# Sigmoid attention and mixture of depths: choosing matmuls moved and halved, values over five gaps, q and k turned behind the outputs

## Chip, cores and metric

One NeuronCore of a Trainium2 chip runs the whole kernel. The metric is the device time of one execution in microseconds. Before the change the median of three runs is 466.48 us (465.75 to 466.99). The execution that the profile shows has a span of 467.6 us.

## What is computed

Eight batches of 448 tokens go through an attention of twelve heads of width 64, in which the softmax is replaced by a sigmoid. The outputs of the heads, side by side, are rows of 768. In each batch the 128 rows with the highest gate score then go through a two-layer network and are added to themselves, weighted by the sigmoid of the score; all other rows pass unchanged.

```python
scores = scale * np.matmul(q, k.transpose(0, 1, 3, 2)) - np.log(S)
attn = 1.0 / (1.0 + np.exp(-scores))
x = np.matmul(attn, v)                  # then (B, H, S, D) -> (B, S, H * D)
...
gate = np.einsum('bsd,d->bs', x, w_gate)
out = x.copy()
for b in range(B):
    top_idx = np.argpartition(-gate[b], capacity)[:capacity]     # capacity = 128
    xe = x[b, top_idx]
    ye = np.maximum(xe @ w1, 0.0) @ w2                           # 768 -> 1024 -> 768
    g = 1.0 / (1.0 + np.exp(-gate[b, top_idx]))
    out[b, top_idx] = xe + g[:, None] * ye
```

Everything is float32.

## The kernel before

**Steps and units.** The 8 x 12 heads are 24 groups of four (`NQ`), taken two at a time in 12 steps `s` (`NS`). Three groups make a batch, so a batch ends in the middle or at the end of a step. A step has seven units `n` (`NU`). A unit (L287) multiplies q and k for a slice of the key tokens, 16 matmuls that the trace records as 32, into two PSUM tiles of two banks each, and ScalarE turns both tiles into the sigmoid (L311). The first matmul of a unit waits until ScalarE has read the tiles' earlier contents. There are four such tiles: two of the pool "psc", and o0 and o1, which collect a step's outputs and are also lent to other work. Some units use o0 and o1 in place of psc (L290): units 1, 3 and 5 of step 0 and unit 4 of steps 1 to 3.

**Values.** `values(s, n)` (L327) is one of four blocks of matmuls that multiply the sigmoids by v into o0 and o1. Blocks 0 and 1 have 64 records, blocks 2 and 3 have 48. Block 0 of step s stands behind the last unit of step s, and blocks 1, 2 and 3 stand behind units 0, 1 and 2 of step s+1. Behind block 3 VectorE transposes the outputs out of o0 and o1 into x_b (`take`, L360, four instructions), which frees the two tiles.

**Order.** The scheduler is manual: each engine executes its instructions in the order in which the Python code emits them. `stream` (L762) emits unit after unit, and `gap(s, n)` (L684) whatever stands behind unit n: value blocks, products of the expert network from the table `WORK` (steps 4 to 11), and what was put off with `put`. TensorE, ScalarE and VectorE each have a queue of this kind; plain loads and stores are issued by SyncE, the scores' and rows' transfers by GpSimd, each in order too.

**VectorE's share.** `turn(i)` (L269) transposes k and q of group i in 32x32 blocks; units 0 to 2 of step s need group 2s, unit 3 and later ones need group 2s+1. `turn(2s+1)` is emitted behind unit 1 of step s, and `turn(2s+2)` behind unit 5. `gates(i)` (L672) multiplies the new outputs by the gate weights and reduces them (L374, L377). When a batch is complete, `gate(b)` (L389) adds this up to one score per token; the scores go to DRAM (L402) and come back spread over all partitions (`spread`, L414). `ranking` (L667) then counts for each token how many are ahead of it (L422, L425) and compares the count with the slot numbers (`place`, L433), which gives the tile `hot`: in column i a one at the token of slot i. In steps 1 to 3 VectorE also makes sums of weight quarters (`make_sum`, L175), for a product scheme with seven products in place of eight.

**Choosing.** `choose(b)` (L438) multiplies `hot`, in four parts of 128 tokens, by `who`, whose two columns hold a token's number and score, into a bank of o0 or o1. Four matmuls (8 records) thus give the token and score of each slot. `fetch` (L447) adds the batch's offset (`idx`, L450), copies the score (`got`, L453) and issues the gather of the 128 rows from DRAM. For batches 0 to 5 this stands behind unit 5 of the step after the one in which the scores were spread; for batch 6 it is in `rest`, the tail behind the last step, ahead of all products there; for batch 7 further down in the tail.

**Fillers.** `keep_busy` (L319) issues four matmuls of no use (three in step 3) behind unit 5 of steps 1 to 3, into the tile that will be o0 of the next outputs.

**Pools of the tail.** `banks("any")` takes tiles of "psc" and of o0 and o1 in turn. A product waits until VectorE or ScalarE has read what its tile held.

Of the kernel before, what the change touches and what calls it, by code (L numbers as in the profile page):

```python
# [17 lines left out]
def kernel(  # L18
# [216 lines left out]
    place_s = const.tile([P, NC], F32, name="place_s")  # L235

    def constants():
        make_identity(nc, iden)
        for a in range(4):
            p = slice(a * TT, (a + 1) * TT)  # L240
            nc.sync.dma_start(
                out=wg_b[p],
                in_=bass.AP(tensor=moe_w_gate.tensor, offset=moe_w_gate.offset + a * TT,
                            ap=[[0, TT], [P, HP], [1, TT]]))
        nc.gpsimd.iota(slots, pattern=[[1, CAP]], base=0, channel_multiplier=0,
                       allow_small_or_imprecise_dtypes=True)

        nc.gpsimd.memset(above, float(S))
        nc.gpsimd.memset(level, 0.0)
        for t in (gate_s, *who):  # L250
            nc.gpsimd.memset(t, 0.0)
        mine = moe.tile([P, NC], F32, name="place")
        for a in range(4):
            nc.gpsimd.iota(mine[a * TT:(a + 1) * TT], pattern=[[1, NC]], base=a * NC,
                           channel_multiplier=TB, allow_small_or_imprecise_dtypes=True)
        every = moe.tile([P, TB, TT], F32, name="rep", bufs=2)
        nc.gpsimd.iota(every, pattern=[[1, TB], [TB, TT]], base=0, channel_multiplier=0,
                       allow_small_or_imprecise_dtypes=True)
        for t in who:
            nc.gpsimd.tensor_copy(t[:, :, 0], mine)  # L260
        for c in range(NC):
            nc.gpsimd.tensor_scalar(
                out=earlier[:, c, :], in0=every.rearrange("p r t -> p (r t)"),
                scalar1=mine[:, c:c + 1], scalar2=None, op0=ALU.is_lt)
# [21 lines left out]

    def unit(s, n):  # L287


        if (s == 0 and n in (1, 3, 5)) or (s in (1, 2, 3) and n == NF + 1):  # L290
            psc = [banks(0), banks(1)]
        else:
            psc = [banks("psc"), banks("psc")]
# [25 lines left out]
    def keep_busy(s):  # L319


        open_outs(s)
        for _ in range(3 if s == 3 else 4):
            nc.tensor.matmul(outs[s][0][:, 0, :HP * TT], iden,  # L324
                             wg_b.rearrange("p h t -> p (h t)"), start=True, stop=True)

    def values(s, n):  # L327
# [11 lines left out]
        if n < 2:  # L339
            at = 4 * (NF - 1)  # L340
            work[at:at] = [(r, None) for r in quads]
        for r, c in work:
            x, pr = divmod(r ^ n, 2)
            rows = slice(r * TT, (r + 1) * TT)
            for j in range(2):
                if c is None:
                    w, a = th[rows, 2 * pr + j, :], attn[s, pr, NF]
                else:
# [3 lines left out]
                                 start=(n == 0 and c == 0), stop=(n == 3 and c == NF - 1))  # L352
        if n < 3:
# [57 lines left out]
    def spread(b, queue=nc.gpsimd):  # L411
        scores = st[b]["scores"]
        rep = st[b]["rep"] = moe.tile([P, S], F32, name="rep", bufs=2)
# [14 lines left out]

    def place(b):
# [6 lines left out]
            in1=place_s.rearrange("p (c o) -> p c o", o=1).to_broadcast([P, NC, CAP]))  # L436

    def choose(b, ps=None):  # L438

        if ps is None:  # L440
            ps = banks("o")[:, 0]
        for c in range(NC):
            nc.tensor.matmul(ps[:CAP, :2], st[b]["hot"][:, c, :CAP], who[b % 2][:, c, :],  # L443
                             start=(c == 0), stop=(c == NC - 1))
        return b, ps

    def fetch(b, ps):  # L447
# [8 lines left out]
        else:  # L456
            xe = moe.tile([P, D], F32, name="xe", bufs=3)
        nc.gpsimd.indirect_dma_start(
            out=xe[:n], out_offset=None, in_=rows_to(b),
            in_offset=bass.IndirectOffsetOnAxis(ap=idx[:n, 0:1], axis=0))  # L460
        st[b].update(idx=idx, xe=xe, picked=got)
# [187 lines left out]
    def routed(b):  # L649
# [14 lines left out]
        if s + 1 < NS:  # L664
            put(s + 1, NU - 2, lambda b: fetch(*choose(b)), b)
# [17 lines left out]

    def gap(s, n):  # L684
        if n < 3 and s > 0:
            values(s - 1, n + 1)
            if n == 2:
                turns[0] = 1
                for i, (m, key) in enumerate(LENT.get(s, ())):
                    lend(m, key, f"d{(s + 1) % 2}{i}")  # L690
                if not turned_next(s):
                    gates(2 * s - 2)
        for item in WORK.get((s, n), ()):
            do(item)
        if n == 3 and turned_next(s):
# [4 lines left out]
        if n == NU - 1 and s < NS:  # L700
            values(s, 0)
        for fn, args in late.pop((s, n), ()):
            fn(*args)
        if n == 3 and s > 0 and not turned_next(s):
# [3 lines left out]
            if waiting:  # L708
                gate(waiting.pop())

    def rest():
# [5 lines left out]
        fetch(*choose(b - 1))  # L717
        for key, slot in (((2, 6), "d10"), ((2, 7), "d11")):
            lend(*key, slot)
        work = [(item, begin(item, "any")) for item in ((1, p, 6), (1, p, 7))]  # L720
        gates(2 * NS - 1)
# [40 lines left out]
    def stream():  # L762
# [14 lines left out]
        for s in range(NS):  # L777
            for n in range(NU):
# [4 lines left out]
                if (n == NU - 1 and s == 0) or (n == 3 and s in (1, 2, 3)):  # L783
                    load_v(s + 1)
                elif n == 3 and s > 4:
                    load_v(s)
                gap(s, n)
                if n == NU - 2 and s in (1, 2, 3):
                    keep_busy(s)
                if n == NU - 2:  # L790
# [9 lines left out]
                if (s, n) == (NS - 1, NU - 1):  # L800
                    for key, slot in (((1, 3), "raw"), ((2, 4), "raw"), ((2, 5), "turned")):
                        lend(*key, slot)
# [34 lines left out]
```

## Time and profile before

| what | us |
|---|---|
| time, median of 3 | 466.48 |
| span in the profile | 467.6 |
| TensorE busy | 451.3 |
| VectorE busy | 293.3 |
| ScalarE busy | 181.8 |
| units (L303), 2,688 records | 170.2 |
| choosing (L443), 64 records | 7.8 |
| fillers (L324), 22 records | 5.4 |
| end of the last matmul, about | 461.6 |

Matmuls are pipelined and overlap, so the time that a group takes of TensorE's path is read better from the distance of the starts than from busy time. In a line of a timeline, the first number is the start in us from the beginning of the span, the second the time taken; an "x4" merges neighbours, and brackets hold the idle time of the engine ahead of the line and what ended it.

### The profile page before, as it was taken

The numbers are of one execution on the slowest core, as the hardware profiler recorded it, in microseconds if no ns is written. First come the engines' busy times: TensorE is split into PE (matmuls) and PEld (weight loads), VectorE is DVE, ScalarE is ACT, GpSimd is POOL, SyncE is SP. The second block draws the span as 40 slices with busy tenths as digits, with TensorE's granted clock in tenths as the row PEclk, the third lists the DMA queues.
The fourth block names the chain that finished last, engine by engine and source line by source line (L and its number), as shares of the span: only waits on it lengthen the run. The fifth ranks groups of instructions, "written<-read, shape, count | busy, mean of one in ns | idle before, by whom it ended". The sixth has DMA issues, their size and how long they took to land.

```text
span 467.6 us, 14444 instructions
## 1 busy us (share of the span) xinstructions
PE 451.3 (97%) x6412; PEld 281.9 (60%) x6412; DVE 293.3 (63%) x631; ACT 181.8 (39%) x237; POOL 32.7 (7%) x54
## 2 busy tenths in 40 slices
PE   8999999979999999999999999999999998999994
PEld 3464745434576755576456764676465738869952
DVE  4308769985642895984643795894742858685372
ACT  3846464624545345324445435324255520102000
POOL 6000000010000000010010000010010001001001
PEclk9999999979999999999999999999999998999998
DMA  8897997989753995994764973993823999611001
GB/s 269 220 313 185 342 347 149 264 197 302 165 193 116 207 192 185 204 215 153 173 227 148 153 202 118 228 213 132 220 102 98 222 181 328 106 34 69 2 0 67
DMA packets 128334, 84.67 MB, mean 181 GB/s; under 512 B 97600, under 2 KB 112064, under 8 KB 128272
## 3 DMA queue, kind: packets, MB, share of 16 engines
q1 hardware_dynamic: 126288, 75.84, 62.2%
q0 software_dynamic: 1984, 7.91, 5.7%
q8 instruction: 50, 0.82, 0.8%
q14 instruction: 12, 0.10, 0.1%
HBM read 63.28 MB, written 20.46 MB: 179 GB/s over the span
## 4 chain that ended last, share of the span: by engine, by line
PE 85%; DVE 8%; DMA 3%; issue 1%; ACT 1%; POOLq 0%; DVEq 0%; ACTq 0%
PE o L351 26%; PE psc L303 23%; PE o L519 13%; PE o L584 11%; PE psc L519 4%; PE psc L584 3%; DVE x_b L366 2%; PE o L303 2%; DMA scores<-total 1%; DVE gate_p L377 1%; DVE scr L374 1%; PE o L775 1%; PE o L443 1%; DMA rep<-scores 1%; PE o L324 1%
## 5 line engine op out<-in xcount | busy, mean ns | idle before, releaser
L303 PE MATMUL psc<-qT,kT 32*64 32x448 f32 x2496 | 155.1, 546 | 0.9 <-ACT attn_u L311 0.9
L311 ACT ACTIVATE attn_u<-psc,bias_s 128x896 f32<-128x896 f32 x86 | 81.9, 1004 | 94.6 <-PE psc L303 94.5
L351 PE MATMUL o<-attn_u,raw_v 32*64 32x448 f32 x960 | 107.8, 536 | 0.8 <-ACT o L354 0.8
L351 PE MATMUL o<-attn_d,raw_v 32*64 32x448 f32 x960 | 106.8, 536 | 0.4 <-ACT o L354 0.4
L303 PEld LDWEIGHTS psc<-qT,kT 32*64 32x64 f32 x2496 | 65.2, 133 | 56.4 <-issue 36.0
L311 ACT ACTIVATE attn_d<-psc,bias_s 128x896 f32<-128x896 f32 x70 | 66.7, 1003 | 47.9 <-PE psc L303 47.9
L366 DVE STREAM_TRANSPOSE x_b<-o 128x448 f32<-128x448 f32 x48 | 26.9, 618 | 81.5 <-PE o L351 77.3
L351 PEld LDWEIGHTS o<-attn_u,raw_v 32*64 32x64 f32 x960 | 45.6, 132 | 20.4 <-issue 12.5
L351 PEld LDWEIGHTS o<-attn_d,raw_v 32*64 32x64 f32 x960 | 43.9, 132 | 18.8 <-issue 14.8
L519 PEld LDWEIGHTS o<-rows_t,w_sb 128*128 128x128 f32 x264 | 30.4, 192 | 4.5 <-issue 1.4
L519 PEld LDWEIGHTS o<-rows_t,attn_d 128*128 128x128 f32 x264 | 30.3, 192 | 3.9 <-DVE scr L374 1.4
L519 PE MATMUL o<-rows_t,w_sb 128*128 128x128 f32 x264 | 31.9, 278 | 0.4 <-DVE rows_t L486 0.3
L519 PE MATMUL o<-rows_t,attn_d 128*128 128x128 f32 x264 | 31.6, 277 | 0.3 <-DVE rows_t L492 0.3
L377 DVE TENSOR_REDUCE gate_p<-scr 128x14 f32<-128x448 f32 x48 | 29.8, 621 | 1.7
L374 DVE TENSOR_TENSOR scr<-x_b,wg_b 128x448 f32<-128x448 f32 x48 | 29.5, 615 | 1.0
L595 DVE SCALAR_TENSOR_TENSOR xe<-o,gate,xe 128x384 f32<-128x384 f32 x37 | 21.1, 611 | 13.4 <-PE o L584 13.3
L278 DVE STREAM_TRANSPOSE kT<-raw_k 128x384 f32<-128x384 f32 x46 | 23.4, 548 | 7.5 <-PE psc L303 3.9
L584 PE MATMUL o<-attn_d,hidden 128*128 128x384 f32 x80 | 27.7, 494 | 0.0
L532 DVE TENSOR_TENSOR hidden<-o,hidden 128x512 f32<-128x512 f32 x24 | 16.0, 687 | 17.9 <-PE o L519 17.7
L535 ACT ACTIVATE hidden<-hidden 128x512 f32<-128x512 f32 x12 | 7.6, 630 | 49.9 <-DVE hidden L532 49.9
L422 DVE TENSOR_SCALAR_CACHE_REDUCE scr<-rep,who 128x448 f32<-128x448 f32 (+1 forms) x32 | 21.5, 671 | 8.6 <-DMA rep<-scores 7.6
L584 PE MATMUL o<-w_sb,hidden 128*128 128x384 f32 x72 | 24.7, 491 | 0.0
(112 smaller groups left out, 476.4 us busy)
## 6 DMA issues: line engine op xcount, KB each, us to landing
attn_d<-sum SPq DMA_DIRECT2D x42, 384.0 KB, 5.5
out_dram<-x_b SPq DMA_DIRECT2D x32, 336.0 KB, 7.7
raw_k<-in_k_dram SPq DMA_DIRECT2D x23, 448.0 KB, 5.3
raw_q<-in_q_dram SPq DMA_DIRECT2D x23, 448.0 KB, 5.9
raw_v<-in_v_dram SPq DMA_DIRECT2D x40, 192.0 KB, 8.1
w_sb<-in_moe_w_dram SPq DMA_DIRECT2D x6, 768.0 KB, 10.9
sum<-hidden SPq DMA_DIRECT2D x6, 768.0 KB, 6.3
rep<-scores POOLq DMA_DIRECT2D x7, 224.0 KB, 4.9
```

The source lines that it names most:

```text
L278: nc.vector.transpose(kT[i][:, e, :HK], sk[:, e, :HK].rearrange("p (m c) d -> p c m d", c=NF))
L303: nc.tensor.matmul(psc[h // 2][y * Dh:(y + 1) * Dh, h % 2, :S], kT[2 * s + x][d, e, r:r + 2, :].rearrange("d r t -> d (r t)"), qT[2 * s + ...
L311: nc.scalar.activation(a, psc[pr][:, :, :S], AF.Sigmoid, bias=bias_s, scale=QK_SCALE)
L351: nc.tensor.matmul(o[x][j * Dh:(j + 1) * Dh, pr, :S], w, a[rows, j, :], start=(n == 0 and c == 0), stop=(n == 3 and c == NF - 1))
L366: nc.vector.transpose(x_tiles[b][:, :, 2 * g + pr, :], outs[s][x][:, pr, :S].rearrange("p (r t) -> p r t", t=TT))
L374: nc.vector.tensor_tensor(out=tmp, in0=x_tiles[b][:, :, hp, :], in1=wg_b[:, hp:hp + 1, :].to_broadcast([P, TB, TT]), op=ALU.mult)
L377: nc.vector.tensor_reduce(out=gate_parts[b][:, :, hp], in_=tmp, axis=AX.X, op=ALU.add)
L422: nc.vector.tensor_scalar(out=junk[:n], in0=rep[:n], scalar1=own, scalar2=0.0, op0=ALU.is_gt, op1=ALU.add, accum_out=above[:n, c:c + 1])
L519: nc.tensor.matmul(ps[:, f, :n], w((t * FH + f) * P, P), x[:, t, :n], start=(t == 0), stop=(t == KH - 1))
L532: nc.vector.tensor_tensor(out=dst, in0=a, in1=b, op=ALU.add)
L584: nc.tensor.matmul(ps[:n, :DH], h[:, t, :n], w(t * DH, DH), start=(t == 0), stop=(t == FH - 1))
L595: nc.vector.scalar_tensor_tensor(out=xe[:n, cols], in0=ps[:n, :DH], scalar=st[b]["gate"][:n, 0:1], in1=xe[:n, cols], op0=ALU.mult, op1=ALU ...
```

## The change

**Fillers.** `keep_busy` is removed.

**Values over five gaps.** In steps 1 to 3 ("early") the first 32 records of block 0 stay behind the last unit of the step whose values they are, its other 32 go behind unit 0 of the next step, and blocks 1, 2 and 3 behind units 1, 2 and 3. The unit that borrows o0 and o1 becomes unit 5.

**q and k.** In steps 1 and 2 `turn(2s+2)` and the load behind it come directly behind the output transposes, ahead of `gates` and `gate`, in step 3 directly behind the fetch of batch 0. All gate work of steps 1 to 3 stands behind unit 4. The v load of the next step moves behind unit 4.

**Choosing moved.** Batch 0 is chosen behind unit 4 of step 3, right behind the output transposes; its gather is issued separately, behind unit 5. Batch 6 is chosen behind products 6 and 7 of the tail, into a tile of "any".

**Choosing halved.** For batches 1 to 5 VectorE adds the four parts of `hot`, each multiplied by its column of `who`, behind `place` (eight instructions of 128x128, two chains of four). Two matmuls with a column of ones, in place of four, then give both columns.

**Buffers.** The spread scores have one buffer in place of two. Two loans of summed weights in step 11 are loaded earlier.

```diff
+    ones = const.tile([P, 1], F32, name="ones")
...
+    def early(s):
+        return 1 <= s <= 3
...
-        if (s == 0 and n in (1, 3, 5)) or (s in (1, 2, 3) and n == NF + 1):
+        if (s == 0 and n in (1, 3, 5)) or (early(s) and n == NF + 2):
             psc = [banks(0), banks(1)]
...
-    def keep_busy(s):
-        open_outs(s)
-        for _ in range(3 if s == 3 else 4):
-            nc.tensor.matmul(outs[s][0][:, 0, :HP * TT], iden,
-                             wg_b.rearrange("p h t -> p (h t)"), start=True, stop=True)
...
+        if part is not None:
+            work = work[8:] if part else work[:8]
...
-        rep = st[b]["rep"] = moe.tile([P, S], F32, name="rep", bufs=2)
+        rep = st[b]["rep"] = moe.tile([P, S], F32, name="rep")
...
+    def added(b):
+        return 0 < b < B - 2
...
+        if not added(b):
+            return
+        st[b]["sums"] = both = moe.tile([P, 2, P], F32, name="sums2")
+        for x in range(2):
+            nc.vector.tensor_scalar(out=both[:, x, :CAP], in0=st[b]["hot"][:, 0, :CAP],
+                                    scalar1=who[b % 2][:, 0, x:x + 1], scalar2=None,
+                                    op0=ALU.mult)
+            for c in range(1, NC):
+                nc.vector.scalar_tensor_tensor(
+                    out=both[:, x, :CAP], in0=st[b]["hot"][:, c, :CAP],
+                    scalar=who[b % 2][:, c, x:x + 1], in1=both[:, x, :CAP],
+                    op0=ALU.mult, op1=ALU.add)
...
+        if added(b):
+            for x in range(2):
+                nc.tensor.matmul(ps[:CAP, x:x + 1], st[b]["sums"][:, x, :CAP], ones,
+                                 start=True, stop=True)
+        else:
+            for c in range(NC):
+                nc.tensor.matmul(ps[:CAP, :2], st[b]["hot"][:, c, :CAP], who[b % 2][:, c, :],
+                                 start=(c == 0), stop=(c == NC - 1))
...
-        if s + 1 < NS:
+        if b == 0:
+            put(s + 1, NU - 1.5, gather, b)
+        elif s + 1 < NS:
             put(s + 1, NU - 2, lambda b: fetch(*choose(b)), b)
...
     def gap(s, n):
-        if n < 3 and s > 0:
+        last = 3 if early(s) else 2
+        if early(s) and n <= last:
+            values(s - 1, n, 1 if n == 0 else None)
+        elif n <= last and s > 0:
             values(s - 1, n + 1)
...
+        if n == last + 1 and s == FIRST:
+            fetch(*choose(0))
+            turn(2 * s + 2)
+            load(2 * s + 4)
-        if n == 3 and turned_next(s):
+        if n == last + 1 and (turned_next(s) or early(s)):
             gates(2 * s - 2)
...
-            values(s, 0)
+            values(s, 0, 0 if early(s + 1) else None)
...
+        if early(s) and n == last and s != FIRST:
+            turn(2 * s + 2)
+            load(2 * s + 4)
...
     def rest():
-        fetch(*choose(b - 1))
         for key, slot in (((2, 6), "d10"), ((2, 7), "d11")):
             lend(*key, slot)
         work = [(item, begin(item, "any")) for item in ((1, p, 6), (1, p, 7))]
+        fetch(*choose(b - 1, bank("any")))
...
-                if n == NU - 2 and s in (1, 2, 3):
-                    keep_busy(s)
-                if n == NU - 2:
+                if n == NU - 2 and not early(s):
                     turn(2 * s + 2)
                     load(2 * s + 4)
```

`FIRST` is 3.

## The prediction

> **What bounds the kernel now.** I read the page's busy shares, then the waits of TensorE, then the timelines of ScalarE and VectorE in steps 1 to 4, then granted clock and busy time in short windows. The page's first two parts:
>
> ```profile
> PE 451.3 (97%) x6412; PEld 281.9 (60%) x6412; DVE 293.3 (63%) x631; ACT 181.8 (39%) x237; POOL 32.7 (7%) x54
> ...
> PE   8999999979999999999999999999999998999994
> ...
> PEclk9999999979999999999999999999999998999998
> ```
>
> TensorE is busy nearly throughout; its hole at slice 8 (93 to 105 us) is also where the granted clock falls. The waits of TensorE name the two holes that matter here:
>
> ```profile
> PE o L324 <- DVE got L453: 3.8, 1, 3.8
> PE o L443 <- DVE x_b L366: 1.5, 1, 1.5
> ```
>
> The first is in step 3: the bank of batch 0's choosing is needed by the filler matmuls (L324), and the two small VectorE instructions that empty it (L450, L453) stand behind all the gate work. The second is in the tail. The clock around both, from the windows (us, TensorE busy, clock, DMA share, GB/s):
>
> ```profile
> 95.00:96.00 1.00, 0.00 (x0) 0.96 0.83 126
> 96.00:97.00 1.00, 0.32 (x1) 0.50 0.94 144
> 102.00:103.00 1.00, 1.00 (x24) 0.62 1.03 190
> 389.00:390.00 1.00, 1.00 (x9) 0.73 0.99 384
> 392.00:393.00 1.00, 1.00 (x7) 0.56 1.02 409
> ```
>
> The clock is halved from 96.0 to 102.8 and from 389.7 to 393.1. The latter made one first-layer product (L519, 24 records) last 4.4 instead of 2.7 us.
>
> Steps 1 to 3 have no expert work, so ScalarE's starts give their rhythm (step 2, units 0 to 6, markers left out):
>
> ```profile
> 50.74 1.90 ACT L311 ACTIVATE attn_d<-psc,bias_s 128x896 f32<-128x896 f32 x2 [1.23 <-PE psc L303]
> 55.25 1.91 ACT L311 ACTIVATE attn_d<-psc,bias_s 128x896 f32<-128x896 f32 x2 [1.26 <-PE psc L303]
> 62.80 1.91 ACT L311 ACTIVATE attn_u<-psc,bias_s 128x896 f32<-128x896 f32 x2 [1.88 <-PE psc L303]
> 65.53 1.91 ACT L311 ACTIVATE attn_u<-o,bias_s 128x896 f32<-128x896 f32 x2 [0.83 <-PE o L303]
> 71.08 1.91 ACT L311 ACTIVATE attn_u<-psc,bias_s 128x896 f32<-128x896 f32 x2 [1.85 <-PE psc L303]
> ```
>
> A unit takes 1.50 us of TensorE, its sigmoid 1.9. Two units in a row on the same two banks are 3.76 us apart (1.9 + 1.5 + about 0.35 of signals); with a full value block (3.0) between, 4.51; the unit that borrows the output banks waits for the four output transposes, 2.73; the next one 1.79. Step 2 lasts 24.90 us, step 3 31.48.
>
> VectorE's own timeline matters most (output transposes, last q transpose before a step's outputs, ranks, comparison that ends the ranking):
>
> ```profile
> 36.58 2.24 DVE L366 STREAM_TRANSPOSE x_b<-o 128x448 f32<-128x448 f32 x4 [13.07 <-PE o L351]
> 57.03 1.07 DVE L285 STREAM_TRANSPOSE qT<-raw_q 128x896 f32<-128x896 f32 x1
> 61.43 2.24 DVE L366 STREAM_TRANSPOSE x_b<-o 128x448 f32<-128x448 f32 x4 [3.33 <-PE o L351]
> 79.33 0.68 DVE L422 TENSOR_SCALAR_CACHE_REDUCE scr<-rep,who 128x448 f32<-128x448 f32 x1
> 86.30 2.24 DVE L366 STREAM_TRANSPOSE x_b<-o 128x448 f32<-128x448 f32 x4
> 106.84 0.68 DVE L422 TENSOR_SCALAR_CACHE_REDUCE scr<-rep,who 128x448 f32<-128x448 f32 x1 [2.32 <-DMA rep<-scores]
> 112.82 0.69 DVE L433 TENSOR_TENSOR hot<-slots,place_s 128x512 f32<-128x512 f32 x1
> ```
>
> From 61.43 to 86.30 it has no idle time: a step's VectorE work, 24.9 us, is as long as the step. So VectorE, not TensorE, sets the pace from step 2 to the outputs of step 3.
>
> **What the Trainium skill says.** "TensorE: Matmul & The Clock Gate", section "What's actually happening", has the clock halved after an idle window of about 3.4 us and restored after a busy one. The trace agrees: low for 3.4 us (389.7 to 393.1) and for twice that (96.0 to 102.8). "DMA: Bandwidth & Descriptors", section "Issuing engines are not separate DMA queues", says that transfers of all issuers share the same engines: the two small score transfers have to share. The trace agrees: the score row took 7.0 us and the spread 4.2 in step 2, 3.5 and 7.8 in step 3. For the new VectorE instructions I use "VectorE: DVE Perf Modes", section on the TRN2 errata: fp32 tensor_tensor takes (N+151)/0.96 ns. At N=512 that is 691; the trace has 687 to 692. At 128 it gives an estimate of 291 ns.
>
> **The change, part by part.**
>
> *Fillers gone* (L324, 22 records): 1.5 us in steps 1 and 2, 2.3 at the low clock in step 3. Steps 1 and 2 become 3.76 (unit 1, now behind only half a block of 1.5) + 4.51 + 3.76 + 3.76 + 2.73 (borrowing moves from unit 4 to 5) + 1.79 + 3.76 (unit 0, behind the other half) = 24.07. That is 0.8 less than 24.90, not 1.5, because half a block does not cover the sigmoid.
>
> *Outputs one gap later.* Step 0's last sigmoid is at 20.11; +3.76 +3.76 +4.51 +3.76 puts unit 3 of step 1 at 35.90, and the value block of 2.25 ends at 38.15. VectorE's transposes start at 38.3, against 36.58. From there to the end of turn(5) the same work stands in the queue, 21.5 us (36.58 to 58.10, 3.04 of it a wait for a store): 59.8. Unit 3 of step 2 needs it and would start at 58.45 (38.15 + 1.50 + 2.73 + 1.79 + 3.76 + 3.76 + 4.51 + 2.25), so TensorE gets a new wait of 1.4. Outputs of step 2: 59.9 + 1.5 + 2.25 + 0.1 = 63.8, against 61.43.
>
> *q and k turned directly behind.* This costs nothing in sum, but moves 2.14 us (43.85 to 45.99) ahead of the gates, so the scores leave 2.14 later. They landed just in time before (79.3), so ranking starts 0 to 2.1 later; I take 1.0. Outputs of step 3: 63.8 + 24.9 + 1.0 = 89.7, against 86.30 and against 87.8 when TensorE would be ready.
>
> *Choosing of batch 0 right behind these outputs.* It starts when the first bank is free, 90.9, takes 0.8, idx and got 0.3 after the transposes end at 91.9: unit 5 starts at about 92.4, where before nothing began before 96.68. Unit 0 of step 4 at 92.4 + 1.5 + 1.79 + 4.56 = 100.3, against 107.12. This is the part that works, 6.8 us on TensorE, if VectorE could follow.
>
> *VectorE up to the outputs of step 4.* Before, from 86.30 to the end of the comparison 113.5, 27.2, of which 2.3 waiting: 24.9 of work. New: the eight sums of batch 1, dependent on each other in two chains; 8 x 0.30 = 2.4 (bounds 1.6 and 2.7). The scores leave 2.4 later behind outputs, so the wait for the spread is 1.3 with short transfers, 4.8 with those of before; I take 2.5. Outputs of step 4: 89.7 + 24.9 + 2.4 + 2.5 = 119.5 (116 to 122), against 117.76. Behind these transposes waits the first row transposition (L480), which needs their bank: 120.7, against 119.05. Before, TensorE idled after it for 1.3 until the sigmoid let unit 4 begin at 121.1; that idle time is gone, so unit 4 begins at about 121.4 in both. But TensorE is now idle from 112.4 to 120.7, the clock falls, and half of one or two windows of 3.4 is lost: 1.7 to 3.4, I take 2.2. Sum of steps 0 to 4: +2.2.
>
> *Choosing halved.* Batches 1 to 5: 8 records in 0.79 become 4, so 0.39 x 5 = 2.0 saved, all on TensorE's path, since steps 5 to 10 are full. Their sums on VectorE lie in its idle time ahead of those steps' outputs (4.8, 6.2, 5.4 and 5.9 us at 183, 220, 289 and 326 us of its timeline).
>
> *Tail.* Choosing of batch 6 goes behind products 6 and 7, so the 1.5 wait and the dip at 389.7 go. But product 5 now lands in the bank that product 6 used, and the addition that empties it (before at 397.04) stands behind idx, which waits for the later choosing: 386.85 + 2.68 + 2.68 + 0.79 = 393.0 instead of 391.63, so the addition ends at 399.2. TensorE is done with product 4 at 395.7. Product 5 starts at 399.4, against 398.96: +0.45, with 3.7 idle in front of it, which more likely than not lowers the clock again (1.7). I take +1.3 in the mean of both.
>
> *Nothing:* the gather of batch 0, the store and loan order, the single spread buffer and the later v loads; each has more than 5 us until its reader.
>
> Sum: +2.2 - 2.0 + 1.3 = +1.5: 466.5 becomes 468.0.
>
> **The rivals.** *Faster, 463:* the store and score transfers land early, because the new order of loads and stores leaves the queues lighter at those moments. Then turn(5) is no wait, the outputs come at 62.5, 87.4 and, with 27.3 of work, 114.7; row transposition at 115.9, unit 4 some 4.8 earlier, less 2.2 for the clock: -2.6; choosing -2.0; tail +0.45, clock kept: -4.2, or 462.3 to 464. For it: a median of 4.1 for the score row over the whole run. Against: in these steps the DMA share is 0.9 to 1.0. *Slower, 472:* the transfers take what they took (7.8), outputs of step 4 at 122: +4.7, tail with two windows of low clock +3: 466.5 + 4.7 - 1.8 + 3 = 472.4. For it: the 7.8 was measured in this very place.
>
> **How the numbers follow.** 0.45 for the worked case (468.0, give or take 1.5), 0.38 for the faster rival, 0.17 for the slower. The bound of 0.3% is 1.4 us: faster takes the first rival nearly whole, 0.38; of the worked case two fifths fall within the bound, 0.19; the rest, 0.43, is slower. The range of 462.8 to 472.0 leaves out the outer part of both rivals.
>
> **What would show it.** The outputs (x_b transposes) of steps 1 to 4 at 38.3, 63.8, 89.7 and 119.5; no filler, unit 5 of step 3 at 92.4; a wait of unit 3 in step 2 for turn(5); low clock around 120 and not from 96 to 102; choosing of 0.4; product 5 of the tail waiting for VectorE with low clock after it. If VectorE idles before the outputs of step 4, waiting for TensorE, the forecast is wrong, and the time near 463.

## The result: 473.0 us, 1.3% slower

The changed kernel takes 473.02 us (median of 4 runs, 470.86 to 473.86), the kernel before, run beside it, 466.74: a ratio of 1.013 (95% interval 1.0092 to 1.0168). The forecast was 468.0 with a range up to 472.0; the rival that came nearest is the slower one (472.4). The traced execution of before was 469.5 us, some 3 us above that kernel's median, so the traces differ by only 4.3 us (spans 467.6 and 471.9) where the timed runs differ by 6.3. The accounting below is that of the traces.

### The profile page after: what moved, and what is told of

Its sections match the earlier page's. It is cut to its first block, busy times and chain, and to the rows that moved or that the text cites. A ratio compares the mean times of both kernels' runs of the same rounds, so it can differ in the third digit from the quotient of the medians.

```text
span 471.9 us, 14407 instructions
## 1 busy us (share of the span) xinstructions
PE 444.7 (94%) x6370; PEld 262.5 (56%) x6370; DVE 306.0 (65%) x671; ACT 182.2 (39%) x237; POOL 32.7 (7%) x55
## 4 chain that ended last, share of the span: by engine, by line
PE 77%; DVE 12%; DMA 7%; issue 2%; ACT 1%; POOLq 0%; SPq 0%; DVEq 0%; ACTq 0%
PE o L352 23%; PE psc L310 22%; PE o L549 12%; PE o L614 11%; PE psc L614 3%; PE psc L549 3%; DMA scores<-total 3%; DMA rep<-scores 2%; DVE x_b L369 2%; DVE gate_p L380 2%; PE o L310 2%; DVE scr L377 2%; DVE scr L428 1%; DVE scr L425 1%; DMA raw_q<-in_q_dram 1%
## 5 line engine op out<-in xcount | busy, mean ns | idle before, releaser
L310 PE MATMUL psc<-qT,kT 32*64 32x448 f32 x2496 | 153.5, 549 | 0.9 <-ACT attn_u L318 0.6
L352 PE MATMUL o<-attn_u,raw_v 32*64 32x448 f32 x960 | 103.6, 535 | 0.8 <-ACT o L357 0.8
L310 PEld LDWEIGHTS psc<-qT,kT 32*64 32x64 f32 x2496 | 60.3, 133 | 64.0 <-issue 42.0
L352 PEld LDWEIGHTS o<-attn_u,raw_v 32*64 32x64 f32 x960 | 41.5, 132 | 24.8 <-issue 19.4
L352 PEld LDWEIGHTS o<-attn_d,raw_v 32*64 32x64 f32 x960 | 40.6, 132 | 20.9 <-issue 17.1
L625 DVE SCALAR_TENSOR_TENSOR xe<-o,gate,xe 128x384 f32<-128x384 f32 x39 | 22.1, 610 | 11.9 <-PE o L614 11.8
L562 DVE TENSOR_TENSOR hidden<-o,hidden 128x512 f32<-128x512 f32 x26 | 17.3, 686 | 17.7 <-PE o L549 17.5
L549 PEld LDWEIGHTS o<-rows_t,w_sb 128*128 128x128 f32 x216 | 25.4, 195 | 4.9 <-issue 2.1
L549 PE MATMUL o<-rows_t,w_sb 128*128 128x128 f32 x216 | 26.9, 282 | 0.4 <-DVE rows_t L516 0.3
```

The source lines that it names most:

```text
L310: nc.tensor.matmul(psc[h // 2][y * Dh:(y + 1) * Dh, h % 2, :S], kT[2 * s + x][d, e, r:r + 2, :].rearrange("d r t -> d (r t)"), qT[2 * s + ...
L352: nc.tensor.matmul(o[x][j * Dh:(j + 1) * Dh, pr, :S], w, a[rows, j, :], start=(n == 0 and c == 0), stop=(n == 3 and c == NF - 1))
L549: nc.tensor.matmul(ps[:, f, :n], w((t * FH + f) * P, P), x[:, t, :n], start=(t == 0), stop=(t == KH - 1))
L562: nc.vector.tensor_tensor(out=dst, in0=a, in1=b, op=ALU.add)
L625: nc.vector.scalar_tensor_tensor(out=xe[:n, cols], in0=ps[:n, :DH], scalar=st[b]["gate"][:n, 0:1], in1=xe[:n, cols], op0=ALU.mult, op1=ALU ...
```

## The profile after

The page's busy shares, its TensorE row and its clock row:

```profile
PE 444.7 (94%) x6370; PEld 262.5 (56%) x6370; DVE 306.0 (65%) x671; ACT 182.2 (39%) x237; POOL 32.7 (7%) x55
...
PE   8999999698299999999999999999999999899994
...
PEclk9999999889589999999999999999999999999999
```

TensorE has 6.6 us less work than before, and the kernel is slower all the same. The hole at slice 8 has become two: a small one at slice 7 (83 to 94 us) and a large one at slice 10 (118 to 130 us), and the low clock has followed both. The waits of TensorE name them:

```profile
PE o L510 <- DVE x_b L369: 10.7, 1, 10.7
PE o L468 <- DVE x_b L369: 3.1, 1, 3.1
PE o L549 <- DVE hidden L562: 2.0, 1, 2.0
```

The filler's 3.8 us wait is gone. In step 4 the row transposition (L510, L480 before) now waits 10.7 us for VectorE to take the outputs out of its bank; the moved choosing of batch 0 (L468) waits 3.1 in the same way. The clock around them, from the windows (us, busy time and instructions of TensorE, its weight loads, VectorE, ScalarE, GpSimd, then clock, DMA share, GB/s):

```profile
92.00:93.00 1.00, 1.00 (x6) 1.00 (x5) 0.26 (x1) 0.00 (x0) 0.00 (x0) 0.50 0.96 148
118.00:119.00 1.00, 0.00 (x0) 0.00 (x0) 0.96 (x3) 0.00 (x0) 0.00 (x0) 0.85 1.31 237
132.00:133.00 1.00, 1.00 (x9) 1.00 (x9) 0.48 (x1) 1.00 (x2) 0.00 (x0) 0.83 0.00 0
```

The clock is at half from about 118.7 to 132.3 (0.85 and 0.83 are the means of the windows in which it changes), so the 5.9 us after TensorE's restart at 126.4 pass at half speed. VectorE's timeline shows why it came so late (output transposes of steps 1 to 4, the first instruction of each ranking, the sums of batch 1's first column):

```profile
38.09 2.24 DVE L369 STREAM_TRANSPOSE x_b<-o 128x448 f32<-128x448 f32 x4 [15.89 <-PE o L352]
62.82 2.24 DVE L369 STREAM_TRANSPOSE x_b<-o 128x448 f32<-128x448 f32 x4 [4.26 <-PE o L352]
83.16 0.68 DVE L425 TENSOR_SCALAR_CACHE_REDUCE scr<-rep,who 128x448 f32<-128x448 f32 x1 [2.52 <-DMA rep<-scores]
90.03 2.23 DVE L369 STREAM_TRANSPOSE x_b<-o 128x448 f32<-128x448 f32 x4
115.70 0.68 DVE L425 TENSOR_SCALAR_CACHE_REDUCE scr<-rep,who 128x448 f32<-128x448 f32 x1 [6.81 <-DMA rep<-scores]
122.41 0.28 DVE L449 TENSOR_SCALAR sums<-hot,who 128x128 f32<-128x128 f32 x1
122.73 1.12 DVE L453 SCALAR_TENSOR_TENSOR sums<-hot,who,sums 128x128 f32<-128x128 f32 x3
125.14 2.24 DVE L369 STREAM_TRANSPOSE x_b<-o 128x448 f32<-128x448 f32 x4
```

VectorE idles 6.81 us for the scores of batch 1, then ranks and sums for 9.4 us, and only then takes the outputs of step 4, which TensorE has had ready since about 114. Before, VectorE had ended the same ranking at 113.5 and then waited for a store of rows, which set the outputs:

```profile
117.76 2.24 DVE L366 STREAM_TRANSPOSE x_b<-o 128x448 f32<-128x448 f32 x4 [4.25 <-DMA out_dram<-x_b]
```

GpSimd's timeline has the two transfers (before, then after):

```profile
95.60 0.53 POOL L402 DMA_DIRECT2D scores<-total  x1 [19.84 <-DVE by_token L404]
99.07 0.56 POOL L414 DMA_DIRECT2D rep<-scores  x1 [2.94 <-DMA scores<-total]
```

```profile
102.62 0.53 POOL L405 DMA_DIRECT2D scores<-total  x1 [22.62 <-DVE by_token L407]
108.31 0.56 POOL L417 DMA_DIRECT2D rep<-scores  x1 [5.16 <-DMA raw_q<-in_q_dram]
```

Before, row and spread together took 106.84 - 95.60 = 11.2 us; after, 115.70 - 102.62 = 13.1: the row 5.7 us instead of 3.5, the spread 7.4 instead of 7.8. (The last bracket names a load of q. The spread has nothing to do with it; it waits for the row, which the trace has landing 5.1 us after its issue.) The row also leaves later behind the outputs of step 3: 12.6 us (102.62 - 90.03) instead of 9.3 (95.60 - 86.30).

## Experiments

They ran on several chips, on which the kernel before took medians of 466.9 to 468.8 us; each ratio is against before on the same chip. My theory after the result: the ranking of batch 1 stands on VectorE ahead of step 4's outputs, so TensorE sits through the wait for the scores. Rivals: the turned order of q and k is the loss; the missing fillers are (the clock falls without them); the eight sums are; the traffic of the stores is.

### The order on VectorE in step 4

**Ranking of batch 1 behind the outputs of step 4.**

```diff
-        put(s + 1, 1, ranking, b)
+        put(s + 1, 2 if b == 1 else 1, ranking, b)
```

> The changed kernel, with the ranking of batch 1 emitted behind the output transposes of step 4 instead of ahead of them. Theory (in VectorE's queue the ranking, waiting for the spread scores, holds up the transposes behind it, and these hold up TensorE): transposes of step 4 at about 114.5 us instead of 125.1, first row transposition at about 116 instead of 126.4, no low clock after 118, time 461 to 464 us (part of the gain may return where choosing of batch 1 waits for the later ranking, about 2 us). Rival (the transposes are late because VectorE has too much work in steps 3 and 4, whatever its order): at most 3 us less than the changed kernel, 470 to 473 us.

Measured: 467.08, ratio 0.9961 (0.9941 to 0.9981), 1.7% better than the changed kernel's 1.013, by one moved call. The waits of TensorE in this kernel:

```profile
PE o L468 <- DVE x_b L369: 4.1, 1, 4.1
PE o L549 <- DVE hidden L562: 2.0, 1, 2.0
PE o L510 <- DMA xe<-out_dram,idx: 1.9, 1, 1.9
```

The 10.7 us are gone, outputs come at 115.71, and the sigmoid of unit 4 starts at 123.01 (131.23 in the changed kernel). So the order on VectorE is what lets the wait reach TensorE. The same order stood in the kernel before and cost less there: the wait was 2.3 us, there were no sums, and a store held the outputs anyway. The gain is smaller than the 461 to 464 us expected, since a smaller wait lies behind it: the gathered rows of batch 0 (1.9). The row transposition came at 119.03 and not at 116, and the clock was low once more, from about 120 to 123.4.

**No sums for batch 1.** Batch 1 is chosen by eight records again; everything else is as changed.

```diff
-        return 0 < b < B - 2
+        return 1 < b < B - 2
```

> The changed kernel, with batch 1 chosen by four matmuls, without sums on VectorE. Theory (the ranking of batch 1 and all behind it are on the path of the end): the 2.7 us of the eight sums come back, 0.4 for the longer choosing is lost, 470 to 471.5 us. Rival (the sums are the whole loss): 466 to 467 us. Second rival (the sums are hidden): 473 us.

Measured: 473.13, ratio 1.0103 (1.005 to 1.0156). Outputs come at 122.95, TensorE waits 7.9 instead of 10.7: the sums are 2.8 of the 10.7 us, no more. The wait for the spread is still 7.07. Unit 4 starts 2.75 us earlier (128.48), but the spans are equal: 1.1 us of this is lost by the end of step 11, and 1.6 in the tail. There product 3 follows the same wait of 2.04 us in both kernels, but here the clock fell after it, and the product took 4.4 us instead of 2.8. Its first line here, to be compared with the last one shown of the changed kernel below (0.71):

```profile
404.12 1.22 PE L549 MATMUL o<-rows_t,raw_k 128*128 128x128 f32 x4 [2.04 <-DVE hidden L562]
```

So in step 4 these sums cost what they take, and the spread's wait remains. In the time of the whole kernel no gain is clear of the noise (1.0103 against 1.013).

**Only the wait taken away.** The ranking of batch 1 counts batch 0's scores once more, so batch 1 picks wrong rows; its own spread still takes place, into a buffer nobody reads.

```diff
-        rep = st[b]["rep"] = moe.tile([P, S], F32, name="rep")
+        rep = st[b]["rep"] = moe.tile([P, S], F32, name="rep") if b != 1 else moe.tile([P, D], F32, name="xe", bufs=3)[:, :S]
...
-        rep = st[b]["rep"]
+        a = 0 if b == 1 else b
+        rep = st[a]["rep"]
...
-        own = who[b % 2][:n, c, 1:2]
+        own = who[a % 2][:n, c, 1:2]
```

> The kernel after, with the order of all instructions kept, but the ranking of batch 1 counts the scores of batch 0 once more, which landed at 83 us, in place of those of batch 1; the spread of batch 1 still takes place, into another buffer that nobody reads. So only the wait for this spread is gone (6.8 us in the trace of the kernel after), and batch 1 picks wrong rows. If this wait is what set the outputs of step 4: they come at 118 to 119 in place of 125.1, unit 4 of step 4 has its sigmoid at 124 to 125.5 in place of 131.2, TensorE waits 3 to 4.5 us for its bank in place of 10.7, and the ratio is 0.997 to 1.002. If another wait of the same length lies behind it (TensorE not ready, the q and k of the next group, the gather of batch 0), the outputs stay after 122 and the ratio stays above 1.006.

Measured: ratio 1.004 (1.0015 to 1.0065), a little above the 0.997 to 1.002 expected. In this trace all of step 3 is 3 us later, so distances count: from the outputs of step 3 (93.11) to those of step 4 (121.30) it is 28.2 us, against 35.1 in the changed kernel. That is 6.9 less, the whole 6.8 of the wait. But TensorE then waited for the gathered rows, as the waits show:

```profile
PE o L511 <- DMA xe<-out_dram,idx: 5.9, 1, 5.9
PE o L469 <- DVE x_b L369: 4.3, 1, 4.3
```

Part of this is my edit's: the gather stood 5.96 us on GpSimd's queue until the unread spread had landed. So I let VectorE read a little of that spread behind the outputs:

```diff
+    def look(b):
+        junk = moe.tile([P, S], F32, name="scr")
+        nc.vector.tensor_copy(junk[:1, :32], st[b]["rep"][:1, :32])
...
         place(b)
+        if b == 1:
+            put(4, 3, look, b)
```

> As the run without the wait for batch 1's spread (its ranking counts batch 0's scores once more, so batch 1 picks wrong rows), with one small VectorE copy behind the outputs of step 4 that reads the unused spread, so that its buffer is released there and the gather of batch 0 isn't held on GpSimd's queue. If the wait for the spread is the cause of the loss: outputs of step 4 about 28.2 us after those of step 3 (35.1 in the kernel after), TensorE waits 3 to 4.5 us for VectorE or for the gather instead of 10.7, unit 4 of step 4 starts 5.5 to 7 us earlier than in the kernel after, and the ratio is 0.997 to 1.001. If the gather takes its place whatever holds it: TensorE waits over 5 us for the rows, and the ratio stays at 1.003 to 1.006.

Measured: ratio 1.0054 (1.0034 to 1.0073), not the 0.997 to 1.001 expected. Outputs again come 27.8 us after those of step 3 (88.64 to 116.48), and the step from unit 3 to unit 4 shrinks from 15.48 to 9.58 us (sigmoids at 114.35 and 123.93). But the gather, issued at 113.08 after 5.2 us on its queue that end with a store of rows, still made TensorE wait 4.8 us. So the spread's wait is worth 5.9 us of TensorE in step 4, and the gather is next in line. Of the loss of 1.3% some 0.8% is then this wait; the ranking and the sums, 9.4 us, still stand ahead of the outputs here.

**Weight sums of step 3 behind the outputs of step 4.** Their two stores of 768 KB, issued at 105.1, run beside the score transfers.

```diff
-            (2, 5): [(2, 5), (2, 6)], (3, 5): [(2, 7), (2, 4)]}
+            (2, 5): [(2, 5), (2, 6)], (4, 2): [(2, 7), (2, 4)]}
```

> The kernel after, with the two weight sums of step 3 (3.5 us of VectorE, two stores of 768 KB that are under way while the scores' row and its spread are) moved behind the outputs of step 4. If these stores slow the two score transfers, these take 9 us in place of 13.1, the spread lands at about 112 instead of 115.7, the outputs of step 4 come at about 121.5, and the ratio is about 1.005. If something else in the traffic slows them (the loads of q, k and v that are issued between 92 and 113 us), the spread lands at 115 or later and the ratio stays 1.011 to 1.014, or is higher, since 3.5 us of work now stand behind the outputs of step 4 where they filled a wait before.

Measured: ratio 1.0243 (1.0209 to 1.0277). Row and spread took 11.0 us (101.96 to 112.99) instead of 13.1. All of it is the spread's (5.4 instead of 7.4); the row took 5.7 as before. So in this trace the stores are 2 us of it. But the 3.5 us of VectorE work, which had filled a wait, now stood behind the outputs: the row buffer that the sums read became free later, and TensorE waited 8.7 and then 3.5 us.

**Stores of batch 1's rows later.**

```diff
-            parts = ((4, 0), (4, 1.5), (4, 3), (4, 4)) if b else (
+            parts = ((4, 3), (4, 4), (4, 4.5), (4, 5)) if b else (
```

> The changed kernel with the stores of batch 1 issued behind units 3 to 5 of step 4 instead of behind units 0 to 4. Theory (the spread of batch 1's scores is slow because the stores with 128-byte pieces share the transfer engines with it): the spread lands 2 to 4 us earlier than 115.7, time 469 to 471 us. Rival (what slows it are the sums of weights and the loads of q and k ahead of the stores): spread within 1 us of 115.7, time 472 to 474 us.

Measured: ratio 1.0166 (1.0111 to 1.0221), spread landed at 116.19, wait 6.14. From row to landing it took 12.4 us (13.1 in the changed kernel). These stores are little or nothing of what slows the spread.

### The turned order of q and k

**`turn` and `load` behind the gates again**, in the changed kernel, then the same with the ranking of batch 1 behind the outputs too:

```diff
             fetch(*choose(0))
-            turn(2 * s + 2)
-            load(2 * s + 4)
...
-        if early(s) and n == last and s != FIRST:
+        if early(s) and n == last + 1:
             turn(2 * s + 2)
```

> The changed kernel, with the q and k transposes of the next step put back behind the gate work of steps 1 to 3. Theory (the wait for the spread scores in step 4 is long because of transfers, not because of the 2.1 us that the scores leave later; TensorE's unit 0 of steps 2 to 4 now waits for its q and k by 1.5 to 4 us): outputs of step 4 within 2 us of 125, time 471 to 475 us. Rival (turning directly behind the outputs is what made the change slower): the scores of batch 1 leave 2 us earlier, time 466 to 469 us.

> The changed kernel with both: ranking of batch 1 behind the outputs of step 4, and q and k turned behind the gate work. Theory (turning directly behind the outputs is worth something once the ranking no longer holds up the outputs): 1 to 4 us more than the kernel with the moved ranking alone. Rival (it only delays the scores): 1 to 2 us less than that kernel.

Measured: ratios 1.0106 (1.0046 to 1.0167) and 1.0119 (1.0051 to 1.0188). Both have this wait of TensorE:

```profile
PE psc L310 <- DVE qT L287: 9.4, 3, 4.6
```

Three units wait 9.4 us for their q, and the first kernel gains nothing although VectorE waits only 1.75 us for the spread there. Against the kernel with the ranking behind alone (0.9961), the second loses 1.6%, more than the 1 to 4 us expected. Turning first isn't the loss; in the new order of values it is needed.

### Parts of the change alone, in the kernel before

**No fillers.**

```diff
-                if n == NU - 2 and s in (1, 2, 3):
-                    keep_busy(s)
```

> The kernel before without the filler matmuls, nothing else changed. Theory (in steps 1 and 2 the fillers lie inside the time that the unit behind them waits for the sigmoid anyway, so they cost nothing; in step 3 they hold TensorE's queue until VectorE has emptied the choosing bank, and without them unit 6 goes ahead): rhythm of steps 1 and 2 unchanged at 3.76 us for units 5 to 6, 2 to 4 us less in step 3, 462.5 to 465 us. Rival (the fillers keep the clock up): low clock in more windows, 467 us or more.

**Choosing halved** for batches 1 to 5 (`added`, the sums in `place`, two matmuls in `choose`, one spread buffer, as in the change).

> The kernel before with the halved choosing alone (sums on VectorE and two matmuls with ones for batches 1 to 5, one spread buffer). Theory (choosing is on TensorE's path in full steps, the sums lie in VectorE's idle time): 0.4 to 0.8 us saved for each of five batches, 463 to 465 us. Rival (the sums of batch 1 delay the outputs of step 4 here too): 466 to 468 us.

**The tail's order.**

```diff
         p, b = NP - 2, B - 1
-        fetch(*choose(b - 1))
...
         work = [(item, begin(item, "any")) for item in ((1, p, 6), (1, p, 7))]
+        fetch(*choose(b - 1, bank("any")))
```

> The kernel before with the moved choosing of batch 6 in the tail alone. As the forecast had it: product 5 waits 3.7 us for its bank, the clock falls again, +0.45 to +2.2, 467 to 469 us. As the trace of the changed kernel now suggests (wait of 2.0 us, clock kept at full): 0.3 to 1.0 us less than before, 465.7 to 466.4 us.

Measured: ratios 0.9966 (0.9934 to 0.9999), 0.9956 (0.9937 to 0.9975) and 0.9996 (0.9972 to 1.002). Without fillers, units 5 and 6 of step 3 are 3.76 us apart instead of 10.04: the fillers' own wait for `got` was the hole, and without them the clock didn't fall there. Little of this reaches the end: counted from the outputs of step 3, unit 0 of step 4 comes 5.7 us earlier, unit 6 only 2.1, because the ranking of batch 1 now waits 4.58 us for its spread ahead of the outputs, and the clock is low from 116.3 to 119.7. With choosing halved alone, the sums of batch 1 cost nothing in step 4: ahead of the outputs VectorE idles 1.53 us instead of 4.25. The tail's order is worth nothing either way; the forecast had a loss. TensorE waits 2.0 us for VectorE there, where it waited 1.5 at another place of the tail before.

**No fillers and choosing halved together:**

> The kernel before, with two parts of the change alone: no fillers, and choosing halved for batches 1 to 5 (with one buffer for the spread). My theory is that these two parts gain and that the new order of steps 1 to 4 loses. Alone they gave -1.5 us (fillers, ratio 0.9966) and -2.0 us (halved, 0.9956), and they act on different waits: the fillers on step 3's hole, the halving on steps 5 to 10, while the eight sums of batch 1 stand in step 4 ahead of the outputs on VectorE in both. If they add up: ratio 0.991 to 0.994, a span of 461 to 462.5, outputs of step 4 at 115 to 117. If the sums of batch 1 eat what the missing fillers gain in step 4: ratio 0.996, outputs of step 4 at 118 or later.

Measured: 467.65, ratio 1.0007 (0.9985 to 1.003). The two gains do not add up. Executions of this kernel ranged from 460.1 to 470.2 us, so the size of the ratio is uncertain: even the eight shortest of the 22 alone would give 0.996, as for either gain by itself, and 0.991 to 0.994 was expected. The traced one is the 460.1 (outputs of step 4 at 114.75, mean clock 0.993), while most others have mean clocks of 0.976 to 0.987. Where the clock falls in those isn't visible in the trace of one that kept it, and stays open.

### The parts together, with the new order on VectorE

**The same, with the ranking of batch 1 behind the outputs of step 4** (the one-line edit shown first):

> The kernel before with no fillers, choosing halved, and the ranking of batch 1 put behind the outputs of step 4 instead of ahead of them. In the run without fillers this ranking waited 4.6 us for its spread ahead of the outputs, and took 6.9 with it. If order is what costs there, the outputs of step 4 come at 103.5 to 106 in place of 115 to 117, limited by TensorE, and some 3 us of the 11 reach the end, because the later gather and the eight sums then stand behind them: ratio 0.984 to 0.990. If TensorE meets another wait in place of it (for the rows of batch 0, which its gather brings), ratio 0.991 to 0.996, like the kernel without this edit.

Measured: 464.29, ratio 0.9956 (0.9934 to 0.9978). No wait for batch 0's rows; but behind unit 5 of step 4 TensorE now meets the sums of batch 1:

```profile
126.71 0.35 PE L463 MATMUL o<-ones,sums 128*128 128x1 f32 x2 [0.45 <-DVE sums L452]
127.98 0.38 PE L463 MATMUL o<-ones,sums 128*128 128x1 f32 x2 [0.91 <-DVE sums L452]
128.29 3.24 PE L305 MATMUL psc<-qT,kT 32*64 32x448 f32 x32
```

The unit after them takes 3.24 instead of 1.76 us: after 2 us with only four small matmuls the clock is halved, at 128.4. Units 5 and 6 are 8.14 us apart (sigmoids at 123.46 and 131.60), but the clock isn't the reason. In ScalarE's queue a relu stands ahead of the sigmoid of unit 6, and it waits for an expert addition on VectorE, behind the ranking, the sums and the gate work:

```profile
131.06 0.63 ACT L559 ACTIVATE hidden<-hidden 128x512 f32<-128x512 f32 x1 [5.70 <-DVE hidden L556]
131.60 1.89 ACT L313 ACTIVATE attn_u<-psc,bias_s 128x896 f32<-128x896 f32 x2
```

**The changed kernel with the ranking behind and the gather of batch 0 directly behind its idx:**

```diff
-        if b:
-            gather(b)
+        gather(b)
...
-        if b == 0:
-            put(s + 1, NU - 1.5, gather, b)
-        elif s + 1 < NS:
+        if b and s + 1 < NS:
```

> The kernel after, with the ranking of batch 1 behind the outputs of step 4, and the gather of batch 0 issued directly behind its idx, at about 93 us, instead of behind the spread of batch 1 (111 us). With the ranking behind alone the ratio was 0.9961, and TensorE waited 1.9 us for the gathered rows. If the gather is what limits step 4 now: no wait for xe, unit 4 of step 4 some 1.5 to 2.5 us earlier, ratio 0.991 to 0.994. If something else ends the wait (the store of rows that the gather reads, or more traffic beside the score row): ratio 0.995 to 0.998.

Measured: ratio 0.998 (0.9957 to 1.0003). The wait for the rows is gone and unit 4 comes 1.3 us earlier behind the outputs of step 3 (30.5 us, 31.8 with the ranking behind alone), but units 5 and 6 are 8.15 us apart (5.82 there), at full clock: TensorE waits 1.4 us for the sums, and 1.0 for an expert addition behind them in VectorE's queue, and ScalarE's relu waits for the same addition:

```profile
133.67 0.63 ACT L564 ACTIVATE hidden<-hidden 128x512 f32<-128x512 f32 x1 [5.70 <-DVE hidden L561]
```

In all four kernels that have the ranking behind and these sums, whatever their clock, the sigmoid of unit 6 comes 17.95 or 17.96 us after the outputs of step 4: VectorE's queue sets it. Hence a last pair, without the sums of batch 1 (the edit `1 < b < B - 2` above), in this kernel and in the one before it:

> The kernel after with the ranking of batch 1 behind the outputs of step 4 and the early gather (ratio 0.998), and batch 1 chosen by eight records as before, without its eight sums. If the sums cost TensorE its time there: no wait for sums (1.4 us) and less than 0.3 for the expert addition behind them (1.0), the choosing itself 0.4 longer, so about 2 us less: ratio 0.992 to 0.995. If they fill time that VectorE has, ratio 0.997 to 1.000.

> The kernel before with no fillers, choosing halved for batches 2 to 5 only, and the ranking of batch 1 behind the outputs of step 4; with the sums of batch 1 too the ratio was 0.9956, and TensorE waited 1.4 us for them. If the sums cost their time: ratio 0.990 to 0.993. If not: 0.995 to 0.998, since the choosing of batch 1 is 0.4 us longer again.

Measured: 463.15, ratio 0.9904 (0.9879 to 0.993), and 460.47, ratio 0.985 (0.9816 to 0.9884). The second is the best of all kernels here. Its TensorE at the place shown above:

```profile
127.40 0.95 PE L467 MATMUL o<-who,hot 128*128 128x2 f32 x8
128.28 1.76 PE L305 MATMUL psc<-qT,kT 32*64 32x448 f32 x32
```

No wait, full clock, units 5 and 6 5.36 us apart. The relu now waits 2.86 us:

```profile
129.53 0.63 ACT L559 ACTIVATE hidden<-hidden 128x512 f32<-128x512 f32 x1 [2.86 <-DVE hidden L556]
```

The eight records cost 0.4 us more than two matmuls would, and the sums that they replace had cost 2.8 (8.14 - 5.36), which is their own time on VectorE. From the outputs to unit 6 it is 15.1 and 15.2 us in this pair. The gain of 1.06% over the version with sums is more than these 2.8 us; the rest isn't located (the traced execution, 464.6, was the slowest of its six).

The pair also bears on a rival that no run tests alone: the values over five gaps and the moved choosing of batch 0. The first kernel has them, with q and k turned behind the outputs and the tail's new order; the second has none of these and is 0.5% faster, though their intervals just overlap. So no gain of these parts is shown.

## Why the prediction was wrong

The sum by its own steps, from the distances between the sigmoids of both traces (after minus before):

| step of the sum | predicted | measured |
|---|---|---|
| steps 0 to 4 (at unit 6 of step 4) | +2.2 | +8.3 |
| choosing of batches 1 to 5 | -2.0 | -3.2, batches 2 to 5 |
| tail (from unit 6 of step 11) | +1.3 | -0.9 |
| sum | +1.5 | +4.3 |

**The step that failed is the wait for batch 1's spread, taken as 2.5 us with an upper bound of 4.8; it was 6.81.** In place of "outputs of step 4: 119.5" they came at 125.14. The working was 2.3 (the wait before) + 2.4 (row sent later) - 2.2 (transfers shorter). Measured: 2.3 + 3.3 (row sent later) + 1.8 (transfers longer, not shorter) - 0.6 (more time on VectorE in front of the ranking). For shorter transfers the forecast had only the row's median of the whole run (4.1 us); the measurement from this place, 3.5 + 7.8 us, was used as the bad end of the range instead of its middle, and the pair of step 2, 7.0 + 4.2, was as long. The row left later than forecast, because VectorE itself waited 0.93 us for the choosing of batch 0, at low clock. The forecast had cited the Trainium skill, "DMA: Bandwidth & Descriptors", section "Issuing engines are not separate DMA queues", for small transfers having to share; the traces fit it (DMA share near 1.0, 13.1 us for a row of 1.8 KB and a spread of 224 KB), and moving two stores away made them 11.0. The mechanism of the slower rival, outputs held by an unchanged transfer, is the one that took place, with a larger size.

From this step follows most of +8.3. The outputs came 5.6 us later than forecast: 4.3 are this wait, 0.3 each the later outputs of step 3 and the longer sums, and 0.7 the rest, mainly VectorE's wait for the choosing. The row transposition at 126.42 instead of 120.7 is the same delay; unit 4 started directly behind it, as predicted. Low clock was taken as 2.2; 5.9 us at half speed are 2.9.

Right, by their numbers:

- Outputs of steps 1 to 3: predicted 38.3, 63.8, 89.7, measured 38.09, 62.82, 90.03.
- VectorE sets the pace up to the outputs of step 4, and low clock comes around 120.
- Eight sums: 2.4 predicted, 2.73 measured (122.41 to 125.14). The estimate of 0.29 us an instruction was made from what the Trainium skill's "VectorE: DVE Perf Modes" (section on the TRN2 errata) has for tensor_tensor, and none of the eight is one: the first of each chain, a tensor_scalar, takes 0.28, the other three, scalar_tensor_tensor, 0.35 each.
- The fillers' hole is gone, and at unit 0 of step 4 the changed kernel is 3.4 us ahead (103.68 against 107.12). All of it is lost again in step 4, nearly all in one wait.

Off in size:

- Unit 3 of step 2 was to wait 1.4 for its q; its sigmoid came 0.6 late, since a store landed 1 us sooner. Step 2 lasts 24.73 us (24.07 and the 1.4 predicted).
- Unit 0 of step 4 was to come at 100.3. The choosing of batch 0 started at 91.35, near the 90.9 forecast, but TensorE had then idled 3.1 us and the clock fell at 91.4, where the forecast had no low clock: the choosing took 1.8 us instead of 0.8 and unit 5 3.29 instead of 1.5. Of this only the 0.9 us that VectorE waited for the choosing reached the outputs of step 4.
- Choosing halved saved more than 0.39 a batch. Its starts are 0.44 us apart to the next unit, where they were 0.88:

```profile
209.79 0.50 PE L464 MATMUL o<-ones,sums 128*128 128x1 f32 x4
```

Steps 6, 7, 9 and 10 became shorter by 1.0, 0.4, 1.0 and 0.7; all other steps from 5 to 11 kept their lengths to 0.02 us. The part above 0.44 lies between the first matmul of unit 6 and its sigmoid (2.44, 1.83, 2.41 and 2.12 us before, 1.83 or 1.84 after); why is not known.

Wrong in place:

- In the tail product 5 was to find product 6's bank not yet emptied, to idle 3.7 us, and the clock to fall. It started directly behind product 4, so it had a free bank. The wait came one product later: product 3, which reads its weights from raw_k and raw_q, waits 2.0 us for an addition that stands behind idx on VectorE, and the clock stayed. The dip at 389.7 is gone, so product 6 takes 2.9 instead of 4.5 us. Products 6, 5 and 3:

```profile
391.90 2.94 PE L549 MATMUL psc<-rows_t,attn_d 128*128 128x128 f32 x24
...
400.94 2.84 PE L549 MATMUL psc<-rows_t,attn_d 128*128 128x128 f32 x24
405.82 0.71 PE L549 MATMUL o<-rows_t,raw_k 128*128 128x128 f32 x4 [2.04 <-DVE hidden L562]
```

But neither dip comes every time, as the last section shows, so the 0.9 gained is that of this pair of traces; alone in the kernel before, the edit gave a ratio of 0.9996.

## What to carry to other kernels

An instruction that frees a bank for another engine should not stand in a queue behind one that waits for a DMA round trip: moving that one ranking behind the outputs was worth 1.7% in the changed kernel, more than all the matmuls the change saved, and 0.5% in the kernel before with its two gains (1.0007 to 0.9956). When a change sends a transfer later into the same traffic, cost its wait with the duration measured in that place plus the delay, and take less only as the good end of the range. Work moved from a full engine to a second one pays where the second idles (batches 2 to 5) and costs where the second sets the pace (batch 1, in step 4: without its sums the two reordered kernels went from 0.998 to 0.990 and from 0.996 to 0.985).

## What was unexpected of the hardware

- Clock. The forecast cited the Trainium skill, "TensorE: Matmul & The Clock Gate", section "What's actually happening", for idle windows of about 3.4 us, and took the length of its low stretch (389.7 to 393.1) as agreement, though that one came after a wait of 1.5 us. After the last unit before the 10.7 us hole (its records end at 115.7) the clock fell at about 118.7, 3.0 us later, and it took 5.9 us of work to come back. The low stretches read from windows are 3.4 us long or multiples of it: 3.4 (128.4 to 131.8 in the kernel of no fillers, halved, ranking behind), 6.8 (91.4 to 98.2) and 13.6 (118.7 to 132.3) in the changed one. But waits shorter than 3.4 us can lower the clock, and not each time. Of the twelve traces of kernels with the tail's new order, all with a wait of 2.04 or 2.05 us, product 3 takes 2.8 us in nine and 4.3 to 4.4 in three; of six traces with the old order and its 1.5 us wait, product 6 takes 2.9 in four and 4.55 in two, the kernel before and the best one among them. The dip that the prediction booked as saved can thus come or not at the same wait, and moves a trace by 1.6 us. At 128.4, in the first kernel named, the clock fell although TensorE was never idle for more than 0.91 us at a time, with four records of one column within 2 us. With the same records and nearly the same waits (0.47 and 0.91 us), the changed kernel with the early gather kept its clock.
- A row of 1.8 KB took 5.7 us and its spread of 224 KB 7.4 us at a DMA share near 1.0, and moving two stores of 768 KB away shortened only the spread, to 5.4 us.
